# A scan and mixture-of-adapters kernel: the expert weights A move to the load queue, and six warm-up matmuls replace ten

## The chip, the cores and the metric

The kernel runs on one core of a Trainium2 chip. The metric is the device time of one execution in microseconds (us). Five executions of the kernel before took 202.69 to 205.0 us, with a median of 204.11.

## What is computed

The reference runs two steps, one after the other. The first is a linear recurrence along the sequence, for each of 8 batches and 128 channels; the second routes each of the 51,200 resulting rows to the two best of eight small adapters and adds what these return.

```python
# a, b: [8, 6400, 128] float32
for t in range(S):
    h = a[:, t] * h + b[:, t]
    out[:, t] = h
x = out.reshape(51200, 128)
logits = x @ w_gate                    # [N, 8]
topk = indices of the two largest logits of a row
w = softmax over these two
delta = sum over the two of  w * ((x @ A[e]) @ B[e])    # A: [8,128,16], B: [8,16,128]
return x + delta
```

The inputs a and b are 26 MB each, the output is 26 MB; the weights are small (A and B have 64 KB each).

## The kernel before, in words

**Tiling.** The 51,200 rows are cut into 100 blocks of 512 rows, called by their number. For block w, the loads `lda` and `ldb` bring rows of a and b into two rings in SBUF with eight places each (`RING`, L302 and L303). Most loads bring two blocks at once (512 KB); a0, b0, b1 and the last a are alone (256 KB). So a1 means the load of blocks 1 and 2 of a, b2 that of blocks 2 and 3 of b, and so on. One load is one DMA, issued by SyncE (SP), in `load` (L454 to L472).

**One block's way.** TensorE (PE) transposes a and b into PSUM (`A0`, `A1` and `AB<w>`, L492). ScalarE (ACT) copies the transposed a to SBUF (`aev<w>`, L526). VectorE (DVE) runs the recurrence over the 512 columns (`scan<w>`, L550) and leaves x, transposed, as 16-bit numbers in `xT`. PE multiplies x by the joined gate and A weights, `cst_h[:, 0:E_A]` (`ZL<k>`, L589), and ACT copies that to SBUF (`zl<k>`, L607). The gating of a group of blocks (L621 and on) finds the two largest logits and makes the weights. GpSimd (POOL) multiplies the products by these weights (`mul<v>`, L766; DVE for some at the end), PE transposes the result (`T<v>`, L774), ACT or DVE copies it (`tev<v>`, L782), PE adds x and the product with B (`D<v>`, L802), ACT or DVE copies this out of PSUM (`oev<v>`, L817), and SP stores two blocks at a time (`st<j>`, L834 and on). A store also waits until the scan of the block 20 further on is done (`HOLD`). The last two blocks have a store each.

**The order.** No engine's order is written by hand. Each operation is given to a planner (`_Plan`, L64) with an engine, an estimated duration, the operations that it waits for and a key. `schedule` (L89) then walks through an estimated time: at each step it takes, of all operations that could start, the one that can start first, and of equals the one with the lowest key. The result is a fixed list for each engine; `run` (L183) issues it, in order, with semaphore waits. An engine whose next operation waits holds up all that stands behind it in its list. The estimates decide nothing but the order.

DMAs share one estimated link in the planner. A DMA (`add_dma`, L336) has an issue time on its engine, a time `ns` on the link and a time `after` until it counts as landed:

```python
if op.dma:
    link = max(link, free[e] + 550.0) + op.dma[2]      # L154, dma[2] is ns
    end[op.name] = link + op.dma[3]                    # L155, dma[3] is after
```

The planner's clock starts at 700 ns for all engines. A load of 512 KB has 1290 ns on the link, one of 256 KB has 690, the gate weights 80, B 220; a load counts as landed 2000 after its time on the link.

**The head.** ACT issues three small loads before its first other work: the gate weights (`wg_in`), B (`B_in`, 128 rows of 512 bytes) and A (`A_in`, L383 to L394). A is stored as expert, channel, rank and is wanted as channel, expert, rank, so its DMA moves 1,024 pieces of 64 bytes. POOL casts each to 16 bits when it has landed (`cstg`, `cstB`, `cstA`, L419 to L432). All `ZL` wait for `cstg` and `cstA`, besides their scans. After its three DMAs, ACT loads its function table (`table`, L396). Meanwhile PE runs ten matmuls of 512 columns on a zeroed tile whose result nobody reads (`heat`, L399 to L404), and after each of the first five `AB<w>` two more of the same (`fill<w>`, L406). SP issues the loads in the order a0, b0, a1, b1, b2, a3, b4, a5, and so on; their key is `w - 2*RING`, less 200 for w up to 3 (L467).

In the profiled execution, PE runs in the head: `heat`, A0, AB0, fill 0, A1, AB1, fill 1, AB2, fill 2, AB3, ZL0, fill 3, ZL1, AB4.

Of the kernel before, what the change touches and what calls it, by code (L numbers as in the profile page):

```python
# [63 lines left out]
class _Plan:  # L64
# [15 lines left out]
    def add(self, name, eng, kind, unit, busy, emit, deps=(), dma=None, mode=None, takes=(), gives=None):  # L80
        self.ops[name] = _Op(name, eng, kind, unit, busy, self.latency, emit, list(deps), dma, mode, takes, gives)
# [118 lines left out]
def bass_associative_scan_2x2__then__mixture_of_adapters_kernel(  # L200
# [19 lines left out]
    RING = CFG["ring"]  # L220
# [68 lines left out]
    with ExitStack() as stack:  # L289
# [36 lines left out]
        def bank(role):  # L326
            return psum[plan.bank_of[role]]
# [6 lines left out]
        add = plan.add  # L334

        def add_dma(name, eng, unit, starts, slot, ns, deps=(), kind="dma", issue=450.0, after=2000.0):  # L336
# [45 lines left out]
        )  # L382
        add_dma(  # L383
            "A_in",
            "act",
            -108,
            [(cst_f[:, E : E + 128].rearrange("d (e r) -> d e r", e=E), moe_A.rearrange("e d r -> d e r"))],
            ("A",),
            700.0,
            (),  # L390
            "fix",
            450.0,
            5500.0,
        )  # L394
        add("w0", "dve", "fix", -109, 60.0, lambda h: h.memset(warm[:, :], 0.0))
        add("table", "act", "fix", -107, 1500.0, lambda h: h.activation(warm[:, :], warm[:, :], ACTF.Sigmoid), ["w0"])  # L396
        add("wt", "dve", "fix", -109, 60.0, lambda h: h.memset(warm_t[:, :], 0.0))

        def heat(h):  # L399
            for _ in range(10):  # L400
                last = h.matmul(bank(("w", -1))[:, :], warm_t[:, 0:128], warm_t[:, :])
            return last

        add("heat", "pe", "fix", -109, 4000.0, heat, ["wt"], mode="half", takes=[("w", -1)], gives=("w", -1))  # L404

        def fill(w):  # L406

# [521 lines left out]
```

## Time and profile before

| | us |
|---|---|
| median of five executions | 204.11 (202.69 to 205.0) |
| the profiled execution's own time | 204.05 |
| its span, from the first instruction to the last | 202.3 |
| PE, ACT, DVE, POOL busy in it | 182.4, 179.2, 171.8, 157.3 |
| A: issued by ACT, landed | 1.66, 12.11 |
| cast of A on POOL | 12.16 to 12.45 |
| first `ZL` on PE | 12.52 |
| first warm-up matmul, first transpose | 1.22, 4.94 |
| last store issued | 198.15 |

All points in time count from the start of the span. The profile has one row for each group of instructions: line, engine, operation, tiles written and read, how often, and the idle time of the engine just before, with the one that ended it. That one is inferred: where an instruction waits for several, the profile names the one that it holds to be the last. Rows of engines marked with a q, as SPq, are issues of DMAs by the engine's sequencer. The row of a DMA's issue ends long before its data lands; the landing is found from the latency that the profile gives for it.

### The profile page before, as it was taken

To read this page: it belongs to the slowest core of one execution; us is meant where nothing else is said; L and a number is where in the kernel's file an instruction comes from. 1 tells how busy PE (TensorE), PEld (TensorE's weight loads), DVE (VectorE), ACT (ScalarE), POOL (GpSimd) and SP (SyncE) were. 2 spreads that over 40 slices of the span, in tenths; PEclk is the share of its full clock that TensorE was granted. 3 is DMA by queue.
4 is the path that set the end of the run, shared out by engine and by line. 5 is a ranking of instruction groups with operands and counts; after the bars stand their busy time and mean duration, and the time that the engine had idled before them with its cause. 6 is when DMAs were issued, how large, how long until landed. Compare 5 with 4: busy or idle time off the path is not lost.

```text
span 202.3 us, 8187 instructions
## 1 busy us (share of the span) xinstructions
PE 182.4 (90%) x3204; PEld 160.7 (79%) x3204; DVE 171.8 (85%) x296; ACT 179.2 (89%) x461; POOL 157.3 (78%) x280
## 2 busy tenths in 40 slices
PE   7779999998998999997999899989999999998770
PEld 3557788887987988896898799879988989897660
DVE  1469999999999899998879888899799699797970
ACT  2259999999998998998999899999999899999761
POOL 2015568889899697888789799999999999769830
PEclk9999999999999999999999999999999999999999
DMA  6999999999999999999999999999999999986985
GB/s 201 366 410 408 409 405 406 405 407 407 406 419 411 413 415 413 412 411 416 411 410 419 405 413 412 417 411 412 416 412 413 412 414 410 395 341 269 403 337 211
DMA packets 23397, 79.30 MB, mean 392 GB/s; under 512 B 3648, under 2 KB 3776, under 8 KB 23360
## 3 DMA queue, kind: packets, MB, share of 16 engines
q1 hardware_dynamic: 22032, 78.65, 97.4%
q8 instruction: 25, 0.41, 0.8%
q10 hardware_dynamic: 1328, 0.14, 0.5%
q14 instruction: 12, 0.10, 0.1%
HBM read 52.56 MB, written 26.21 MB: 390 GB/s over the span
## 4 chain that ended last, share of the span: by engine, by line
PE 46%; ACT 20%; DVE 10%; issue 7%; DMA 6%; POOL 6%; SPq 2%; DVEq 0%; POOLq 0%
PE ps L492 17%; PE ps L802 14%; PE ps L589 7%; PE ps L774 7%; DMA b_in<-in_b_dram 6%; DVE xT L550 6%; ACT zl L607 6%; ACT a_st L526 6%; POOL zw L766 5%; ACT outt L817 5%; SPq L345 2%; ACT pn L656 2%; DVE zw L766 2%; DVE zwT L782 1%; ACT g L745 1%
## 5 line engine op out<-in xcount | busy, mean ns | idle before, releaser
L550 DVE TENSOR_TENSOR_SCAN xT<-a_st,xT,ps 128x512 f16<-128x512 f32 x96 | 120.2, 1252 | 13.1 <-ACT a_st L526 6.5
L766 POOL TENSOR_TENSOR zw<-zl,g 128x512 f16<-128x512 f32 x93 | 98.7, 1068 | 8.3 <-ACT g L745 8.2
L607 ACT COPY zl<-ps 128x408 f32<-128x408 f32 (+1 forms) x139 | 71.2, 538 | 1.6 <-PE ps L589 1.6
L492 PE MATMUL ps<-ident_f,a_in 64*128 64x64 f32 (+1 forms) x792 | 66.9, 228 | 4.0 <-DMA b_in<-in_b_dram 1.0
L526 ACT COPY a_st<-ps 128x512 f32<-128x512 f32 x100 | 61.2, 637 | 10.0 <-PE ps L492 9.3
L492 PE MATMUL ps<-ident_f,b_in 64*128 64x64 f32 (+1 forms) x792 | 67.1, 228 | 1.7 <-issue 1.6
L492 PEld LDWEIGHTS ps<-ident_f,a_in 64*128 64x128 f32 (+1 forms) x792 | 56.0, 138 | 14.0 <-issue 4.4
L817 ACT COPY outt<-ps 128x512 f32<-128x512 f32 x99 | 60.5, 627 | 2.9 <-PE ps L802 2.3
L492 PEld LDWEIGHTS ps<-ident_f,b_in 64*128 64x128 f32 (+1 forms) x792 | 55.8, 139 | 1.2 <-issue 0.9
L589 PE MATMUL ps<-cst_h,xT 128*128 128x136 f16 x400 | 49.0, 233 | 1.6 <-DVE xT L550 1.5
L802 PE MATMUL ps<-ident_h,xT 128*128 128x128 f16 x400 | 42.9, 229 | 2.3 <-issue 1.3
L774 PE MATMUL ps<-ident_h,zw 128*128 128x128 f16 x400 | 38.7, 220 | 4.2 <-DVE zw L766 2.3
L589 PEld LDWEIGHTS ps<-cst_h,xT 128*128 128x128 f16 x400 | 35.4, 148 | 5.6 <-DVE xT L550 2.1
L782 DVE COPY zwT<-ps 128x256 f32<-128x256 f32 x89 | 35.8, 409 | 3.5 <-PE ps L774 3.3
L802 PE MATMUL ps<-cst_h,zwT 128*128 128x128 f16 x400 | 38.7, 219 | 0.0
L802 PEld LDWEIGHTS ps<-ident_h,xT 128*128 128x128 f16 x400 | 33.2, 148 | 4.7 <-DVE zwT L782 1.9
L774 PEld LDWEIGHTS ps<-ident_h,zw 128*128 128x128 f16 x400 | 25.2, 98 | 7.7 <-DVE zw L766 3.2
L802 PEld LDWEIGHTS ps<-cst_h,zwT 128*128 128x128 f16 x400 | 27.2, 99 | 0.0
L656 ACT ACTIVATE pn<-d 128x96 f32<-128x96 f32 (+2 forms) x72 | 22.9, 328 | 0.1
L735 POOL TENSOR_TENSOR um<-d,pn 128x96 f32<-128x96 f32 (+2 forms) x36 | 14.1, 394 | 5.6 <-ACT pn L656 4.8
L706 POOL TENSOR_TENSOR L<-zl,pn 128x96 f32<-128x96 f32 (+2 forms) x34 | 13.3, 394 | 3.6 <-ACT pn L656 3.0
L728 POOL TENSOR_TENSOR d<-d 128x96 f32<-128x96 f32 (+2 forms) x38 | 13.8, 365 | 1.4 <-DVE d L681 0.5
(31 smaller groups left out, 85.7 us busy)
## 6 DMA issues: line engine op xcount, KB each, us to landing
a_in<-in_a_dram SPq DMA_DIRECT2D x49, 512.0 KB, 15.8
b_in<-in_b_dram SPq DMA_DIRECT2D x49, 512.0 KB, 15.6
out_dram<-outt SPq DMA_DIRECT2D x49, 512.0 KB, 15.5
a_in<-in_a_dram SPq DMA_DIRECT2D x2, 256.0 KB, 9.2
b_in<-in_b_dram SPq DMA_DIRECT2D x2, 256.0 KB, 4.4
out_dram<-outt SPq DMA_DIRECT2D x2, 256.0 KB, 3.6
cst_f<-in_moe_B_dram ACTq DMA_DIRECT2D x1, 64.0 KB, 3.5
cst_f<-in_moe_A_dram ACTq DMA_DIRECT2D x1, 64.0 KB, 10.4
```

Source lines behind the costliest of these rows:

```text
L492: last = h.transpose(*args())
L526: lambda h: h.copy(a_st[w % NAS][:, :], bank(("a", w))[:, :]),
L550: last = h.tensor_tensor_scan(out=x_at(lo, hi), data0=a_st[w % NAS][:, lo:hi], data1=bank(("b", w))[:, lo:hi], initial=init, op0=ALU.mult, ...
L589: last = h.matmul(dst, x_block((b0 + j) // Q, (b0 + j) % Q), wA_h)
L607: return h.copy(zl[:, r0 : r0 + n, :], src)
L656: lambda h: h.activation(v(pn[s]), v(src[s]), ACTF.Relu, bias=bias, scale=scale),
L735: lambda h: h.tensor_tensor(out=v(um[s]), in0=v(d1[s]), in1=v(pn[s]), op=ALU.subtract),
L766: lambda h: h.tensor_tensor(out=oview, in0=zview, in1=gview, op=ALU.mult),
L774: last = h.transpose(dst[:, q * 128 : (q + 1) * 128], zw[v % NZW][:, q, :], ident_h[:, :])
L782: return copy(zwT[v % NZT][:, :].bitcast(F32), bank(("O", v))[:, 0 : UT // 2])
L802: last = h.matmul(bank(("O", v))[:, cols], (x_block(v, q), zwT[v % NZT][:, cols])[part], (ident_h[:, :], Bcat_h)[part], start=part == 0 an ...
L817: return copy(outt[:, v % NOUT, :], bank(("O", v))[:, :])
```

## The change

A is no longer issued by ACT but by SP, in its row of loads. The key puts it between b1 and b2, so it is SP's fifth DMA. The planner is told that A takes 1200 ns on the link instead of 700, and that it counts as landed 2000 after that instead of 5500. The warm-up has six matmuls and not ten, with 2600 ns in the plan instead of 4000. ACT keeps the DMAs of the gate weights and of B. The five fills and all else stay as they are in the program, but the planner makes the order of every engine anew from these numbers.

```diff
         add_dma(
             "A_in",
-            "act",
-            -108,
+            "sp",
+            1.5 - 2 * RING - 200,
             [(cst_f[:, E : E + 128].rearrange("d (e r) -> d e r", e=E), moe_A.rearrange("e d r -> d e r"))],
             ("A",),
-            700.0,
+            1200.0,
             (),
             "fix",
             450.0,
-            5500.0,
+            2000.0,
         )
...
         def heat(h):
-            for _ in range(10):
+            for _ in range(6):
                 last = h.matmul(bank(("w", -1))[:, :], warm_t[:, 0:128], warm_t[:, :])
             return last
...
-        add("heat", "pe", "fix", -109, 4000.0, heat, ["wt"], mode="half", takes=[("w", -1)], gives=("w", -1))
+        add("heat", "pe", "fix", -109, 2600.0, heat, ["wt"], mode="half", takes=[("w", -1)], gives=("w", -1))
```

## The prediction

> **What bounds the kernel now.** I read the page first, then the stretches of busy time, the waits and the timeline of the first 20 us, and last the stores at the end.
>
> ```profile
> PE 182.4 (90%) x3204; PEld 160.7 (79%) x3204; DVE 171.8 (85%) x296; ACT 179.2 (89%) x461; POOL 157.3 (78%) x280
> DMA  6999999999999999999999999999999999986985
> q10 hardware_dynamic: 1328, 0.14, 0.5%
> PE 46%; ACT 20%; DVE 10%; issue 7%; DMA 6%; POOL 6%; SPq 2%; DVEq 0%; POOLq 0%
> ```
>
> The engines and the DMA are both nearly full (the 40 slices fall under 9 in the first and the last few alone), and the chain of waits runs mostly through PE. So the stages have to be told apart; the columns are the stretch, its length, PE, PEld, DVE, ACT and POOL busy, the clock, the DMA share and GB/s:
>
> ```profile
> 20.00:172.00 152.00, 144.44 (x2683) 131.05 (x2682) 138.90 (x226) 146.14 (x374) 134.64 (x231) 1.00 1.03 411
> 172.00:186.00 14.00, 13.35 (x223) 11.99 (x222) 12.12 (x22) 13.75 (x39) 11.16 (x22) 1.00 0.83 332
> 186.00:202.30 16.30, 8.66 (x125) 7.13 (x121) 9.58 (x26) 9.27 (x28) 6.95 (x12) 1.00 0.81 320
> ```
>
> From 20 to 172 us the DMA engines work without a hole at 411 GB/s, and at that rate the 79.3 MB of the page take 193 us by themselves. PE and ACT are 95% and 96% busy beside them. After 20 us the waits name no load. Compute and transfers thus run side by side, and the last stores tell which of them sets the end.
>
> ```profile
> 193.74 0.33 SPq L345 DMA_DIRECT2D out_dram<-outt  x1
> 196.28 0.33 SPq L345 DMA_DIRECT2D out_dram<-outt  x1
> 197.46 0.33 SPq L345 DMA_DIRECT2D out_dram<-outt  x1
> 198.15 0.33 SPq L345 DMA_DIRECT2D out_dram<-outt  x1
> ...
> out_dram<-outt SPq DMA_DIRECT2D x2, 256.0 KB, 3.6
> ```
>
> With their single latencies (5.48, 3.56, 3.64 and 3.59 us) they land at 199.22, 199.84, 201.10 and 201.73: steps of 0.62, 1.26 and 0.63 us for 256, 512 and 256 KB, which is 416 to 423 GB/s, the full rate again. The trace's landing marks (one for each of the 16 DMA engines) say that one engine is late: the first mark of the last store is at 200.6, the last at 201.73, and the slowest engine is behind in this way all through the run. So the end belongs to the slowest DMA engine, and compute has about 1.1 us of slack behind it.
>
> **Where A hurts.** Its row, with the neighbours in time:
>
> ```profile
> 11.35 0.58 ACT L526 COPY a_st<-ps 128x512 f32<-128x512 f32 x1 [0.79 <-PE ps L492]
> 12.16 0.29 POOL L430 CAST cst_h<-cst_f 128x128 f16<-128x128 f32 x1 [7.14 <-DMA cst_f<-in_moe_A_dram]
> 12.52 0.21 PEld L589 LDWEIGHTS ps<-cst_h,xT 128*128 128x128 f16 x2 [1.35 <-DVE xT L550]
> 12.90 0.39 ACT L607 COPY zl<-ps 128x272 f32<-128x272 f32 x1 [0.97 <-PE ps L589]
> 13.35 0.13 PEld L492 LDWEIGHTS ps<-ident_f,a_in 64*128 64x128 f32 x1
> ```
>
> A is issued at 1.66 and lands 10.4 us later, at 12.11. The cast follows, and 0.07 us after it the first products (ZL0). The page puts PE's idle 1.35 us down to the scan, but scan 1 ended at 9.69; the cast of A was the last. PE stood still from 11.3 to 12.5, with ZL0 in front and AB4 (at 13.35, its load in since 11.90) behind.
>
> **The change, part by part.** The sum is made against the profiled execution: 204.05 us, its span of 202.3 and 1.75 around it; the median of the runs shown is 204.11.
>
> *A's bytes.* They are neither more nor fewer. Priced by the dip in the transfers where A's pieces ran:
>
> ```profile
> 5.00:6.00 1.00, 1.00 (x10) 0.90 (x9) 0.00 (x0) 0.43 (x1) 0.01 (x1) 1.00 1.19 288
> 6.00:7.00 1.00, 0.50 (x3) 0.10 (x2) 0.73 (x1) 0.16 (x1) 0.00 (x0) 1.00 1.10 310
> 7.00:8.00 1.00, 0.89 (x11) 0.76 (x12) 0.49 (x1) 0.35 (x1) 0.00 (x0) 1.00 1.04 401
> ```
>
> (411-288)+(411-310) = 224 KB not moved, or 0.54 us; from above, the whole queue q10 (gate, B, A) took 0.5% of 202.3 = 1.0 us. Today these lie beside the loads; after, in their row, ahead of b2. Before and after, every engine moves them once: 0. What no row shows is 1,024 pieces of 64 B inside SP's queue; I bound it by 0.5 us either way (the dip avoided, or paid a second time) and take 0.
>
> *When A lands.* Loads a1 and b1 landed at 6.86 and 7.67 with A beside them; without, up to 0.54 earlier. A follows b1 by 0.54 to 1.0: 7.7 to 8.7, I take 8.3, so cast at 8.65. ZL0 then waits for scan 1 alone, which ends at 9.2 to 9.7. The far end is today's latency from the new issue at 2.54: 12.9.
>
> *SP.* One more issue ahead of b2, some 0.45 us (the row of each early issue), so all later loads are issued 0.45 us later. b2 landed 6.6 us after its issue and the queue only deepens (12.8 us for the load issued at 5.79): hidden by the queue; without that cover, 0.45. ACT loses its third issue: the table load starts at 1.7 in place of 2.15; ACT's next work is at 5.57: 0.
>
> *PE's order.* The planner is given A at 6560+2000 = 8560 (its link sum: a0 2390, gate 2470, b0 3160, B 3380, a1 4670, b1 5360) where it had 5370+5500 = 10870. So ZL0 and ZL1, ready with scan 1 at some 9540 of the plan, come before AB2 (b2 at 9850) and no longer behind AB3. These figures give the order, not a time. On the chip: ZL0 at about 9.4, ZL1 to 9.9, AB2 then at 9.9 in place of 9.22 (0.7 later, with aev2 and scan 2 behind it, now 10.65), AB3 0.5 later, and AB4 at 12.1 instead of 13.35. Scan 4 (14.78, after which DVE is full) moves to about 13.9. What is late next is load b8, which lands at 18.54 and holds AB8 at 18.59; there the scans lose part of the lead. Of 1.2 us I leave 0.8 to products, gating and ACT (full from 20 to 50 us); ends 0 and 1.2.
>
> *Six warm-ups.* Ten took from 1.22 to 4.94; six at 0.43 end at 3.8. a0 landed at 3.71 and b0 at 4.49, so A0 and AB0 can run up to 1.1 and 0.8 us sooner, and scan 0 (6.27) with them. A1 waits for a1 at 6.86 (6.3 after): 0. If the clock stays low longer, the row is the warm-up itself: 634 ns median for it, 379 for the same matmul at L411. PE's 3.7 us of work between 4.9 and 9 (0.60+0.60+0.59+0.71+0.66+0.59 in the timeline) could then take up to 634/379 times as long until the clock comes; most of it fills waits for a1 and b1, and AB1 alone (0.66) and A1 (0.71) move what follows, by some 0.7; scan 1 stays under today's 9.69 plus 0.2, and ZL0 still comes ahead of 12.5. Price 0, ends 0 and 0.7.
>
> The Trainium skill, "TensorE: Matmul & The Clock Gate" (Part 1, the HAM clock gate), speaks against this part: the clock is released after about 3.4 us of sustained activity, counted in free-running windows. By it six warm-ups fall short of a window and ten fill one; AB0 and AB1 would run slow and the sum would be 0.2 to 0.7 us longer in the head. The fall from 634 to 379 ns some 3 us after the first warm-up agrees with the rule; no row shows six.
>
> *To the end.* Compute arrives 0.8 us sooner, but the last three landings follow each other at transfer speed: the slowest engine is not sooner. 0 if it binds as here, 0.8 if it does not; I take 0.2. 204.05 - 0.2 = 203.85, against the median: 203.9.
>
> **The rivals.**
> 1. *The lead is carried to the end*: the constant 3.6 us of the last three stores is a latency and no queue. For it: 15 engines were through up to 1.1 us sooner, and the DMA share after 186 us is 0.81. Against it: steps of exactly 0.62, 1.26, 0.63. Time 204.1 - 0.8 to 1.2 = 203.1, and about 201.9 where the slowest engine is 1.0 less behind too.
> 2. *A late in front of AB2* (the other side): PE works in order, and ZL0 now stands before AB2. It begins with A landing after 9.0 and shows in the time from about 10.2 on, when the 1.1 us of slack are gone. At the far end of 12.9, ZL0 starts at 13.3 and AB2 moves from 9.22 to 13.8; scan 2 follows 1.4 later at 15.2, scans 2 and 3 and the maxima take 3.1, so scan 4 moves from 14.78 to 18.3, and DVE is full after that. 3.5 us, less 1.1: 206.5. For it: A's 10.4 us now. Against it: those were spent beside SP's whole row of loads, while b1, issued in that row at 2.10, took 5.6.
> 3. *The new order is worse further on*: the greedy planner takes all later choices anew. A block costs about 1.8 us of PE (182.4/100); one block's work more exposed at the end, less 1.1 of slack, is +0.7: 204.8; two, +2.5: 206.6. The 7% of issue on the chain shows that order has such a price; nothing shows its sign.
> 4. *Nothing happens in the head either*: A as late, AB2 not blocked: 204.1, inside the forecast.
>
> **How the numbers follow.** Forecast with rival 4: 0.46, own range 203.2 to 204.6. Rival 1: 0.24, of which 0.13 under -1%. Rival 3: 0.17, of which 0.08 over +1%. Rival 2: 0.13, of which 0.08 over. About 1% (202.1 and 206.2) is what a measurement here can tell from no change. Faster 0.13 + 0.02 from the forecast's edge = 0.15; slower 0.08 + 0.08 and 0.03 from the forecast's other edge = 0.19; same 0.66. Range: from rival 1's lower end to rival 3's upper, 202.0 to 206.3.
>
> **What would show it.** Right: A lands at 7.7 to 8.7, ZL0 starts at 9.2 to 9.9, AB4 by 12.3, L401's median stays near 634 and L411 near 379, the last three landings stay 0.6, 1.3, 0.6 apart. Wrong: PE idle before ZL0 past 10.2 with AB2 behind it (rival 2); L411 in the first 10 us over 500 ns (clock); last store issued over 1.1 us after 198.15 (rival 3); an end that moves with the last issue (rival 1); holes in the transfers between 3 and 12 us, which would price A in SP's queue over my 0.5.

## The result, and the profile after

The changed kernel took 203.88 us in the median of 43 runs (203.01 to 207.73), the kernel before, beside it, 203.29 us in 80 runs (202.48 to 207.54). The ratio is 1.0021, with a 95% interval of 1.0005 to 1.0038: by the ratio 0.2% or 0.4 us slower. Times here and below are medians of all executions, while a ratio compares only executions in the faster of two states that the chip shows, and so need not be the quotient of two medians. The profiled execution after took 203.69 us with a span of 201.9.

The head did what the change says, and more. From the trace's timeline (start, duration, engine, line):

```profile
2.57 0.43 SPq L345 DMA_DIRECT2D cst_f<-in_moe_A_dram  x1
7.36 0.29 POOL L430 CAST cst_h<-cst_f 128x128 f16<-128x128 f32 x1 [2.33 <-DMA cst_f<-in_moe_A_dram]
9.04 0.35 PE L589 MATMUL ps<-cst_h,xT 128*128 128x136 f16 x2 [1.03 <-DVE xT L550]
13.78 1.26 DVE L550 TENSOR_TENSOR_SCAN xT<-a_st,xT,ps 128x512 f16<-128x512 f32 x1
```

A landed 4.7 us after its issue, at 7.31 instead of 12.11. ZL0 now waits for scan 1 (`xT L550`), no longer for A. Scan 4 (the last line) started 1.0 us sooner than before.

The end did not come sooner. The page:

```profile
PE 183.7 (91%) x3200; PEld 162.4 (80%) x3200; DVE 171.3 (85%) x294; ACT 180.7 (89%) x463; POOL 158.1 (78%) x280
...
PEclk9999999999969999999999999999999999999998
DMA  6999999999999999999999999999999999987977
...
q8 instruction: 25, 0.41, 0.8%
q10 hardware_dynamic: 288, 0.07, 0.2%
...
PE 44%; ACT 17%; DVE 11%; DMA 8%; POOL 7%; issue 7%; SPq 4%; POOLq 1%; ACTq 0%; DVEq 0%
```

Queue q10 has lost A (1328 packets before, 288 now). New is the 6 in the clock's row, at 55 to 60 us. The long stretch is as full as it was (the stretch, its length, PE, PEld, DVE, ACT, POOL, clock, DMA share, GB/s):

```profile
20.00:172.00 152.00, 145.31 (x2666) 131.78 (x2665) 137.94 (x225) 145.65 (x370) 133.88 (x229) 0.99 1.03 412
172.00:186.00 14.00, 12.98 (x216) 11.61 (x213) 13.19 (x22) 13.71 (x37) 11.09 (x20) 1.00 0.82 327
186.00:201.90 15.90, 8.45 (x128) 7.26 (x125) 8.13 (x25) 9.80 (x30) 7.65 (x14) 0.96 0.84 329
```

The last stores show that the bound has changed:

```profile
195.97 0.33 SPq L345 DMA_DIRECT2D out_dram<-outt  x1
197.36 0.33 SPq L345 DMA_DIRECT2D out_dram<-outt  x1
197.85 0.35 SPq L345 DMA_DIRECT2D out_dram<-outt  x1
198.34 0.67 SPq L345 DMA_DIRECT2D out_dram<-outt  x1
```

They landed at 198.63, 200.03, 200.70 and 201.37, after 2.67 to 3.03 us, and all 16 DMA engines were done with the last one within 0.2 us. Before, the last store was issued at 198.15, took 3.59 us, and one engine came 1.1 us after the first. So the slow DMA engine no longer holds the end; compute does, and it issued its last store 0.19 us later than before. The lead of the head (scan 10 started 1.02 us sooner, scan 20 0.70; scans are counted from 0 as DVE runs them, and four blocks have two) is not there at the end. Where it went can't be read scan by scan against before: the two orders place the scans differently, and from scan 30 on the difference swings between 1.60 us sooner and 2.30 late. Comparisons within one order, further down, are steady. In the chain of waits from 50 to 62 us (start, length, what):

```profile
53.53 1.51 PE ps L492 x39
55.04 1.45 issue
56.49 0.52 PE ps L492 x9
```

PE stood for 1.45 us in the middle of one AB, between two transposes of the same block, where the program has no wait.

### The profile page after: what moved, and what is told of

It is laid out like the page before. It is cut to its first block, busy times and chain, and to the rows that moved or that the text cites. A ratio compares the mean times of both kernels' runs of the same rounds, so it can differ in the third digit from the quotient of the medians.

```text
span 201.9 us, 8170 instructions
## 1 busy us (share of the span) xinstructions
PE 183.7 (91%) x3200; PEld 162.4 (80%) x3200; DVE 171.3 (85%) x294; ACT 180.7 (89%) x463; POOL 158.1 (78%) x280
## 4 chain that ended last, share of the span: by engine, by line
PE 44%; ACT 17%; DVE 11%; DMA 8%; POOL 7%; issue 7%; SPq 4%; POOLq 1%; ACTq 0%; DVEq 0%
PE ps L492 16%; PE ps L802 13%; DVE xT L550 8%; PE ps L589 8%; DMA a_in<-in_a_dram 8%; PE ps L774 7%; ACT outt L817 5%; ACT zl L607 5%; POOL zw L766 5%; ACT a_st L526 4%; SPq L345 4%; ACT pn L656 2%; ACT g L745 1%; DVE zwT L782 1%; POOLq L289 1%
## 5 line engine op out<-in xcount | busy, mean ns | idle before, releaser
L550 DVE TENSOR_TENSOR_SCAN xT<-a_st,xT,ps 128x512 f16<-128x512 f32 x96 | 120.2, 1252 | 10.5 <-ACT a_st L526 5.8
L607 ACT COPY zl<-ps 128x408 f32<-128x408 f32 (+1 forms) x139 | 73.1, 536 | 2.8 <-PE ps L589 2.4
L492 PE MATMUL ps<-ident_f,a_in 64*128 64x64 f32 (+1 forms) x792 | 68.0, 230 | 2.5 <-DMA a_in<-in_a_dram 1.1
L492 PE MATMUL ps<-ident_f,b_in 64*128 64x64 f32 (+1 forms) x792 | 68.3, 230 | 1.4 <-issue 1.4
L492 PEld LDWEIGHTS ps<-ident_f,a_in 64*128 64x128 f32 (+1 forms) x792 | 56.6, 140 | 11.6 <-issue 3.3
L817 ACT COPY outt<-ps 128x512 f32<-128x512 f32 x100 | 61.3, 624 | 2.8 <-PE ps L802 1.7
L492 PEld LDWEIGHTS ps<-ident_f,b_in 64*128 64x128 f32 (+1 forms) x792 | 56.7, 140 | 2.2 <-issue 1.9
L589 PE MATMUL ps<-cst_h,xT 128*128 128x136 f16 x400 | 50.7, 235 | 1.9 <-DVE xT L550 1.5
L589 PEld LDWEIGHTS ps<-cst_h,xT 128*128 128x128 f16 x400 | 36.4, 148 | 5.9 <-DVE xT L550 2.6
L698 POOL TENSOR_TENSOR d<-zl,m 128x96 f32<-128x96 f32 (+2 forms) x34 | 11.7, 343 | 4.1 <-DVE m L691 3.8
```

Source lines behind the costliest of these rows:

```text
L492: last = h.transpose(*args())
L550: last = h.tensor_tensor_scan(out=x_at(lo, hi), data0=a_st[w % NAS][:, lo:hi], data1=bank(("b", w))[:, lo:hi], initial=init, op0=ALU.mult, ...
L589: last = h.matmul(dst, x_block((b0 + j) // Q, (b0 + j) % Q), wA_h)
L607: return h.copy(zl[:, r0 : r0 + n, :], src)
L817: return copy(outt[:, v % NOUT, :], bank(("O", v))[:, :])
```

## The experiments

Each ratio is against the kernel before, run beside it on the same chip. "Old order" means that all engines keep the order of the kernel before, "new order" that of the changed kernel.

### The transfers, the warm-ups and the order apart

One line at the end of `schedule` moves A between queues and leaves the order of everything else. In the old order:

```diff
+        self.order["act"].remove(ops["A_in"]); self.order["sp"].insert(4, ops["A_in"]); ops["A_in"].eng = "sp"
...
-            for _ in range(10):
+            for _ in range(6):
```

`oldorder_sp_6` has both edits, `oldorder_sp_10` the first alone, `oldorder_act_6` the second alone.

> The old order of every engine, with A's DMA moved to SP as its fifth and six warm-ups: the change without the planner's new order. Theory O (the new order loses the lead of the head): A lands at about 7.3 as in the changed kernel, PE does not stop before the first products, and the lead of up to 1 us stays: 0.2 to 0.6% faster than before (ratio 0.994 to 0.998). Rival Q (A in SP's row of loads costs): as slow as the changed kernel or slower, ratio 1.002 or more. Rival W (six warm-ups cost): the same 1.002, with slow matmuls in the first 10 us. If the end belongs to the slowest DMA engine alone: 1.000.

> The old order with A's DMA on SP and the ten warm-ups kept. Theory O: as the run with six warm-ups, ratio 0.994 to 0.998, since the first transposes wait for load a1 anyway. Rival W: faster than the one with six by 0.2% or more. Rival Q: 1.002 or more.

> The old order with A on ACT as before, and six warm-ups. Theory O: 1.000 (0.999 to 1.001), the first transposes start 1 us sooner and wait for load a1 again. Rival W: 1.002 or more, with the clock low in parts of the first 10 us.

Measured: 203.12 us (ratio 0.9972, 0.9934 to 1.001), 202.98 (0.9977, 0.9939 to 1.0015) and 203.02 (0.9974, 0.9931 to 1.0017). Neither A's 1,024 pieces in SP's row nor the six warm-ups cost anything that can be measured, and both at once bring no gain that can be either: all three intervals hold 1. `oldorder_sp_10` shows why: it issued its last store at 197.03, 1.1 us sooner than before, but that store took 4.5 us and landed at 201.53, 0.2 us sooner. (`oldorder_act_6` differs here: issued 1.32 us sooner than before, its last store landed 1.29 us sooner, with one engine 1.15 us behind the first.) The page of `oldorder_sp_10`, KB and us from issue to landing:

```profile
out_dram<-outt SPq DMA_DIRECT2D x2, 256.0 KB, 4.5
```

The new order with the old transfers, A third on ACT and ten warm-ups:

```diff
+        self.order["sp"].remove(ops["A_in"]); self.order["act"].insert(2, ops["A_in"]); ops["A_in"].eng = "act"
...
-            for _ in range(6):
+            for _ in range(10):
```

> The changed kernel's order of every engine, but A issued by ACT as its third DMA and ten warm-ups: the new order without the change. A lands at about 12 and the first products, now ahead of block 2's transposes on PE, start at about 12.5; block 2's transposes start at 13 instead of 9.2. Theory O: slower than before by the order's cost (0.2%) and by the stop of PE, less what the slack takes: ratio 1.005 to 1.015. Rival Q or W: no worse than 1.000 to 1.005, since neither A in SP's row nor six warm-ups are in it.

Measured: 210.88 us, but with runs from 203.29 to 212.08, so that no interval is given. A took 11.0 us on ACT's queue and landed at 12.71:

```profile
12.76 0.29 POOL L430 CAST cst_h<-cst_f 128x128 f16<-128x128 f32 x1 [7.51 <-DMA cst_f<-in_moe_A_dram]
13.20 0.42 PE L589 MATMUL ps<-cst_h,xT 128*128 128x136 f16 x2 [4.04 <-POOL cst_h L430]
```

PE stood for 4.04 us with ZL0 in front and AB2 behind it, and then ran at half its clock (same columns as above; the clock is third from the end):

```profile
13.20:19.00 5.80, 5.80 (x56) 3.83 (x58) 2.65 (x6) 2.65 (x7) 0.70 (x3) 0.50 1.02 409
```

This is rival 2, and PE's stop in the head is real. What it costs is not measured: the profiled execution (212.08 us) is the longest of the six, another took 203.29, and the same order with ten warm-ups and A early (`neworder_sp_10`, below) took 206.7 by itself.

### What the planner is told

The same program, where A's `after` is 2000 (the changed kernel once more), 3000, 3900 or 4600. Only the order differs; 4600 gives the old order, and so the same program as `oldorder_sp_6`.

```diff
-            2000.0,
+            3000.0,
```

> The changed kernel unaltered, beside three that differ from it in one number of the planner alone. Theory O (the new order loses the head's lead): 1.002 against before, and 0.3 to 0.6% slower than told_4600, whose DMAs and matmuls are the same. Rival Q (A in SP's row of loads costs): all four of this call at 1.002 or more. Rival N (nothing but the run's scatter): all four alike within 0.2%.

> The changed kernel with the planner told that A lands 3000 after its time on the link and not 2000: same DMAs, same instructions; the order of PE has block 2's transposes ahead of the first products, and everything later is planned anew. Theory O in its narrow form (what costs is the head, the first products ahead of block 2): as told_4600, 0.997. Theory O in its wide form (each order has its own pauses far behind the head): a value of its own between 0.995 and 1.005, that need not lie between its neighbours'.

> As before with 3900: block 2's transposes and its two fills ahead of the first products, block 3's behind. Narrow form: as told_4600, 0.997. Wide form: a value of its own between 0.995 and 1.005.

> As before with 4600: the planner then gives every engine the very order of the kernel before, so that this is the change without a new order (the program of oldorder_sp_6, measured once more beside the changed kernel). Theory O: 0.995 to 0.999, faster than after_again by 0.3 to 0.6%, the lead of about 1 us kept to the last store's issue wherever the clock stays full. Rival Q or N: as after_again, 1.002.

Measured: 203.70 (1.0032, 1.0 to 1.0064), 203.81 (1.0011, 0.9987 to 1.0035), 206.41 (1.0134, 1.0088 to 1.018) and 203.32 (1.0004, 0.998 to 1.0028). With equal work and equal transfers, an order alone came to ratios of 1.0004 to 1.0134; only `told_3900`, outside both its expectations, is clear of the others, and between the changed kernel's repetition and `told_4600` the intervals overlap. In the profiled execution of `told_3900` (209.42 us, the longest of its six), PE paused for 1.59 us at 17.3 (for a load of b), and for 1.54 and 1.51 us at 79.2 and 95.6, and stretches at half clock followed the first two.

### Does the slowest DMA engine hold the end?

Stores 12, 20, 28 and 36 are cut to 64 columns (the rest of their rows is not written); this takes 1.97 MB, or 4.8 us at 411 GB/s, off the DMA engines and nothing off compute. The edit, in the kernel before, in `told_4600` and in the changed kernel:

```diff
+            if j in (12, 20, 28, 36):
+                rows, tile = rows[:, 0:64], tile[:, 0:64]
```

> The kernel before, with four of its 51 stores (j = 12, 20, 28, 36) cut from 1024 to 64 columns; the rest of those rows is not written. Orders of all engines are before's. It spares the DMA engines 1.97 MB, 4.8 us at 411 GB/s, and no engine of compute anything. If the slowest DMA engine sets the end of before and compute has 1.1 us of slack behind it, the time falls by 0.5 to 1.1 us and not by 4.8, and the last store then lands under 3.1 us after its issue. If compute sets the end already, it stays within 0.3 us.

> Before's order with A in SP's row and six warm-ups, and the same four stores cut to 64 columns. Its profile without the cut had the last store issued 3.0 us sooner than before and landed 1.1 us sooner. If the slowest DMA engine holds the end there, the time falls by 1 to 2.5 us against its own 203.1 to 203.3 and comes out at 200.5 to 202.3, ratio 0.985 to 0.994. If the end is set by compute and the late engine only goes with it, it stays at 203.

> The changed kernel (new order) with the same four stores cut to 64 columns. If its end is set by compute, as the late issues and the latencies of 2.7 to 3.0 us in its two profiles say, it stays at 203.4 to 203.9, ratio 1.001 to 1.003, and the gap to before's order with the same cut opens from 0.4 to 1 us or more. If the DMA engines set its end, it falls by 1 to 2 us too.

Measured: 202.83 us (0.9937, 0.9897 to 0.9976), 200.64 (0.9867, 0.9821 to 0.9913) and 203.73 (0.9981, 0.9942 to 1.0019). `told_4600` is the clear case; its last store without and with the cut:

```profile
195.18 1.24 SPq L345 DMA_DIRECT2D out_dram<-outt  x1
...
195.12 0.33 SPq L345 DMA_DIRECT2D out_dram<-outt  x1
```

The first landed at 200.59, the second at 197.73. First the page without the cut:

```profile
out_dram<-outt SPq DMA_DIRECT2D x2, 256.0 KB, 5.4
```

and with it:

```profile
out_dram<-outt SPq DMA_DIRECT2D x2, 256.0 KB, 2.3
```

Its scans start within 0.1 us of each other in the two, from scan 38 to the last. So compute had 3 us of lead at its end, and the slowest DMA engine (2.7 us behind the first without the cut) kept 2.9 of them. `before_light` landed 1.37 us sooner than before, 0.97 of it from a latency of 2.62 for 3.59: the slack of about 1.1 us that I had read from before was there.

`after_light` was to stay at the time of the changed kernel. The gap to the old order of `told_4600` did open, from 0.2 or 0.3% to 1.1% (0.4% to `before_light`): with the load taken off the DMA engines, the new order's compute is the later one. But it fell a little too, and its trace shows one reason: its last store was issued at 195.92, 2.4 us sooner than in the changed kernel. (This profiled execution, 201.42 us, is the fastest of twelve, which go up to 204.86.) From 50 to 75 us, the first of PE's waits in the changed kernel (us in all, times, longest):

```profile
PE ps L492 <- issue: 1.4, 1, 1.4
PE ps L774 <- issue: 0.7, 1, 0.7
PE ps L492 <- ACT zl L607: 0.3, 1, 0.3
```

and in `after_light`:

```profile
PE ps L589 <- ACT outt L817: 0.9, 1, 0.9
PE ps L774 <- issue: 0.6, 1, 0.6
PE ps L492 <- ACT zl L607: 0.3, 1, 0.3
```

The pause of 1.45 us is missing, and it had come before any cut store (the first was issued at 87.7 us). Of five profiles of this program's order with six warm-ups and whole fills, four have the pause at 55 us, of 1.43 to 1.45 us; `after_light` alone does not. These five have one order, so their scans can be compared one by one. Against `after_light`, the changed kernel is 0.06 us late at scan 29 (50.4 us), 2.32 at scan 39 (68.1 us) and 2.43 at the last; its repetition is 0.13, 2.11 and 2.17 late. Nearly the whole loss falls at the pause and in the 12 us behind it.

### What the pauses are

From 45 us on and up to the last stretch, PE's pauses of over 0.6 us lie at fixed places in its list. Counted in recorded matmuls, the changed kernel has them at 838 and 1087, its repetition at 838 and 962; before at 715, 963, 1460, 1833; `told_3900` at 964, 1088, 1212, 1460 (put down to a scan), 1584, 2330. That is every 123 to 125 matmuls, or a multiple. Old and new orders share these places, and four warm-ups more do not move them: before, with ten, has its pause at 715 inside the 457th matmul of L492, `oldorder_act_6`, with six, at 715 inside the 461st. The page shows 25 packets of kind "instruction" with 0.41 MB, 16 KB each, over 3,200 recorded matmuls with a weight load each: 128 to a packet. In the changed kernel one packet's transfer ends at 55.14, and the pause runs from 55.04 to 56.49; in `told_3900` packets end at 79.41 and 95.78, and the pauses run from 79.21 to 80.75 and from 95.64 to 97.15. The same holds throughout: over all twenty profiles, 47 pauses of more than 0.6 us between 45 and 186 us have no releaser named, and every one ends 1.20 to 1.62 us after the end of such a packet's transfer. So I took the pauses for PE waiting for its next 16 KB of instructions. If that is so, more matmuls in the head move the places in the work. First, the changed kernel with ten warm-ups and the plan of six:

```diff
-            for _ in range(6):
+            for _ in range(10):
```

> The changed kernel with ten warm-ups in the program, while the planner keeps the 2600 ns of six: the orders of all engines stay the changed kernel's. If the order is what costs, it stays at 203.6 to 204.0, ratio 1.001 to 1.004. If the six warm-ups cost, it falls to before's 203.3 or under. PE has four instructions more ahead of everything; if PE's pause of 1.4 us at 55 us, seen in both profiles of the changed order, belongs to the place in PE's list of instructions, it moves by some matmuls or stays within 1 us of 55; if it is chance, it is gone.

Measured: 206.7 us (1.0165, 1.0116 to 1.0215), a miss: the order is the changed kernel's, and A is early. PE's pauses in its timeline:

```profile
56.55 0.27 PE L492 MATMUL ps<-ident_f,b_in 64*128 64x64 f32 x1 [0.95 <-issue]
...
64.52 0.38 PE L802 MATMUL ps<-cst_h,zwT 128*128 128x128 f16 x4 [1.05 <-issue]
...
72.60 0.27 PE L802 MATMUL ps<-cst_h,zwT 128*128 128x128 f16 x2 [1.11 <-issue]
80.41 0.21 PE L492 MATMUL ps<-ident_f,a_in 64*128 64x64 f32 x1 [1.62 <-issue]
```

They come after matmuls 838, 962, 1087 and 1211 of PE's list. The first is at the 520th matmul of L492 and no longer at the 524th: four more warm-ups, four matmuls earlier in the work, and the same place in the list. After the fourth pause, the clock was at half from 81.7 to 85.1. By scan 50 (88.9 us) this run was 3.35 us behind before and 2.40 behind the changed kernel, which has its order.

Two kernels tried to take load off the DMA engines altogether, with stores 0 to 43 cut (`if j < 44`; the rest of those rows is not written):

> The changed kernel with stores 0 to 43 cut from 1024 to 64 columns; the rest of those rows is not written, the last seven stores are whole. Orders of all engines are the changed kernel's. It takes about 21 MB of 79 off the DMA engines and nothing off compute. Theory: PE's pauses are late fetches of its instructions, which wait behind data in the DMA engines; with a quarter of the data gone, the pauses at the fetches (55.0, 63.6, 71.6 us) shrink under 0.4 us, no stretch at half clock follows, and the last store is issued at 193 to 196 in place of 198.3. Rival: the planner's order is worse by what waits for what; then the last store stays over 1 us later than in before's order with the same cut.

> Before's order with A in SP's row and six warm-ups, and the same stores 0 to 43 cut to 64 columns (the rest of those rows is not written). If fetches and the clock make the difference between the two orders, its last store is issued within 0.7 us of that of the changed kernel with the same cut; if the order itself does, it is issued 1 to 2.5 us sooner than there.

Measured: 205.86 us (1.0138, 1.0087 to 1.0189) and 201.33 (0.9866, 0.9811 to 0.9921), four runs each. The first expectation fell: with a quarter of the bytes gone, the pause at 838 is still 1.45 us, and the last store was issued at 198.14, against 198.34 whole. So compute, and not the amount of data, sets that order's last issue; that the packets wait behind the stores' data is not borne out. Its last three stores then took 4.4 to 4.7 us to land, which I can't explain. The profile of `old_fewstores` has 6.83 us at half clock from 7.9 us on and is not compared; the times of the two, 4.5 us apart, say again that without the stores' load the new order is the slower one.

Next, 64 empty instructions ahead of PE's list, in the changed kernel and in `told_4600`:

```diff
+        for _ in range(64 if eng == "pe" else 0):
+            handle.nop()
```

> The changed kernel with 64 empty instructions ahead of PE's list; orders and work are the same, but every later place in PE's instruction memory moves by 64 instructions. If PE's pauses are fetches of 16 KB, they stay at fixed distances in the list and so come some 24 to 32 matmuls (1 to 2 us of work) earlier in the work: the pause after PE's matmul 838 goes, and there is one at about 806 to 814. The time changes with it, by up to 3 us either way. If the pauses belong to the work (a wait in the order that the profile does not show), they stay at 838 and 962 and the time at 203.7 to 203.9.

> Before's order with A in SP's row and six warm-ups, and the same 64 empty instructions ahead of PE's list. If the place of the fetches in the work decides what an order costs, this one's time of 203.1 to 203.3 may rise too, to as much as 206; if before's order bears any place of them because compute leads the DMA engines by 1 to 3 us, it stays at 202.9 to 203.5.

Measured: 204.24 us (1.0031, 0.9995 to 1.0068) and 203.29 (1.0016, 0.9985 to 1.0048). The pause of 1.45 us stayed at matmul 838 and at the same transpose. By the expectation that speaks for a wait that belongs to the work; but the packets also end at the same matmuls as before (838, 957, 1079 beside 838, 959, 1079 in the repetition), so nothing was moved, and whether the empty instructions reached PE's memory no row shows. The two tell nothing about the pauses. So the last pair moves real matmuls: in the five fills, eight of 128 columns replace two of 512.

```diff
-                for _ in range(2):
-                    last = h.matmul(bank(("w", w))[:, :], warm_t[:, 0:128], warm_t[:, :])
+                for i in range(8):
+                    last = h.matmul(bank(("w", w))[:, 0:128], warm_t[:, 0:128], warm_t[:, 0:128])
```

> The changed kernel; each of the five fills has eight matmuls of 128 columns in place of two of 512, so 30 matmuls more on PE in the head for the same columns; orders as in the changed kernel. If PE's pauses are its 16 KB instruction packets, they stay at PE's matmuls 838, 962, 1087 of the list, which are then 30 matmuls earlier in the work (the pause now inside the 524th matmul of L492 comes at its 496th to 508th), and with another place the time may leave 203.9: 202.9 to 206.7. If they belong to the work, they stay at the 524th matmul of L492, and the time at 203.7 to 203.9.

> Before's order with A in SP's row and six warm-ups, and the same five fills of eight matmuls of 128 columns. Its compute is 3 us ahead of before at the last store and the DMA engines end it, so pauses that move should not show: 202.9 to 203.5. If the place of the packets decides for this order too, it goes to 204 or more.

Measured: 203.82 us (1.0027, 0.9993 to 1.006) and 204.47 (1.0051, 1.0018 to 1.0085). In the profiles the roles are exchanged; in the times, the old order lost (1.0051, where it stood at 1.0004 and 0.9972 with whole fills), but the new one did not gain. In the new order the pause at 55 us is gone. PE's waits of that kernel from 50 to 86 us begin with:

```profile
PE ps L492 <- issue: 0.5, 1, 0.5
```

It issued its last store at 196.05, and the DMA engines ended it (4.63 us to land, the slowest engine 1.8 behind). The old order got the pauses, after matmuls 840, 1088 and 1336; they stand in its chain of waits:

```profile
54.04 1.42 issue
...
69.27 1.37 issue
...
83.34 1.74 issue
```

`told_4600` had one pause of 0.69 us in that stretch, and was 2.04 us ahead of before at scan 50; this one was 2.75 us behind, and issued its last store at 198.34 in place of 195.18. Against `told_4600`, which has the same order, its scans are 0.76 us late ahead of the first of these pauses, 2.0 behind it, 3.0 behind the second and 4.8 behind the third. The places in PE's list are those of all other kernels (840 is within the few records that a trace lacks), and the work at them is other work. This shows that the pauses go with PE's list of instructions and not with the order's waits. That they are the packets' landing rests on the spacing and the times given above. From the start of a packet's transfer to the end of the pause, the 47 took 2.27 to 2.65 us, so a packet comes late when its transfer starts with less work than that left in front of its place: at matmul 815 to 819 for place 838 in the four profiles with the pause, at 788 in `after_light`. What sets the start is open.

Ten of the profiles together, with the start of a scan less that of before, and the last store (for the kernels with the new order, the scans 40, 50 and last compare only with each other):

| kernel | scan 10 | scan 20 | scan 40 | scan 50 | last scan | last store issued | landed |
|---|---|---|---|---|---|---|---|
| before | 0 | 0 | 0 | 0 | 0 | 198.15 | 201.73 |
| changed | -1.02 | -0.70 | -0.03 | +0.94 | +0.08 | 198.34 | 201.37 |
| changed, again | -0.68 | -0.35 | -0.24 | +0.67 | -0.19 | 198.09 | 201.12 |
| `after_light` | -0.73 | -0.43 | -2.35 | -1.43 | -2.35 | 195.92 | 198.95 |
| `after_fill8` | -0.27 | -0.12 | -2.27 | -2.60 | -2.23 | 196.05 | 200.68 |
| `neworder_sp_10` | -0.02 | -0.02 | +0.04 | +3.35 | +2.71 | 200.98 | 204.01 |
| `told_4600` | -1.53 | -1.28 | -1.92 | -2.04 | -2.95 | 195.18 | 200.59 |
| `oldorder_sp_6` | -1.38 | +0.30 | +0.74 | +0.62 | -0.15 | 197.99 | 201.17 |
| `oldorder_act_6` | -0.75 | -0.74 | -0.46 | -0.58 | -1.32 | 196.83 | 200.44 |
| `old_fill8` | -1.22 | -0.40 | +0.07 | +2.75 | +0.24 | 198.34 | 201.57 |

`oldorder_sp_6` and `told_4600` are one and the same program. The first paused for 1.12 us at 18.05 (for a load of a), ran at half clock from 20.9 to 24.3 and paused for 1.13 us at matmul 715, where the second did not; its last store was issued 2.8 us later and landed 0.6 us later. So one profile is not its kernel: a single execution of the same program moves by nearly as much as the orders differ, and in the old order most of that is hidden at the end.

## Why the prediction was right and where it was wrong

**Right: the head.** A was to land at 7.7 to 8.7 and landed at 7.31, just ahead of the range. ZL0 was to start at 9.4 (9.2 to 9.9) and started at 9.04, AB4 at 12.1 and started at 12.14, scan 4 at 13.9 and started at 13.78. AB2 was to be held until 9.9 and came at 9.32. Where these differ, the chip was sooner: a1 landed 1.0 us and b1 0.8 us earlier than before. That this is due to A, which no longer ran beside them, is not shown: over all profiles a1 landed at 5.7 to 7.9 us with A in SP's row and at 6.1 to 7.2 with A on ACT.

**Right: A's bytes, SP and the warm-ups at 0.** Three kernels in the old order stand at 0.997 with these edits, and a repetition of the one with both at 1.0004. The Trainium skill's "TensorE: Matmul & The Clock Gate" (Part 1, the HAM clock gate) spoke against six warm-ups. The clock did come later, at 5.9 us instead of 4.4 in the two profiles, and the first fill matmul took 558 ns, over the 500 that I had set as a sign; the other nine took 379 to 390. Over all profiles the full clock came at 4.2 to 7.2 us with six warm-ups and at 4.4 to 6.6 with ten. `oldorder_act_6` has the six alone, with its first two fill matmuls at 634 ns, and shows no cost.

**Right for the old order: the slowest DMA engine.** A lead of 1.1 us at the last issue gave 0.2 us at the end (`oldorder_sp_10`), one of 3.0 gave 1.1 (`told_4600`), and without the four stores 2.62 us of lead over `before_light` gave 2.63. `oldorder_act_6` kept its 1.32 all the same: in the old order the slowest engine is 0.6 to 2.7 us behind, from one profile to the next, so rival 1, the lead carried to the end, is weakened and not out. In the changed kernel the sign failed: the last landings are 1.40, 0.67 and 0.67 apart, and not 0.6, 1.3 and 0.6, as they follow issues 1.39, 0.49 and 0.49 apart.

**Wrong: the lead of 0.8 us after load b8, and with it "to the end I take 0.2".** I let compute keep 0.8 us and asked only whether the DMA engines would take it. In the profile, compute kept nothing. It lost 2.4 us at and after the pause at matmul 838 (last issue 198.34 against 195.92 without it). The DMA engines by themselves end at 200.6 (`told_4600`, `after_fill8`; 200.4 to 201.7 in others that they end), and a last store in this order takes 3.0 us to land, so compute binds from an issue at 197.6 on: 1.7 us of slack without the pause, 0.7 too late with it. The old order of `told_4600` needs 2.6 us for its last store and so binds from 198.0 on; issued at 195.18, it has 2.8 us and can bear one such pause, as `oldorder_sp_6` did. So the sign was missed: rival 3, the new order worse further on, is what happened, at +0.4 us where I had priced it at +0.7. Its cause was not the one that I named. I spoke of a block's work more exposed by the planner's later choices, about 1.8 us; what the profiles show is PE's list with other work at the places where PE stops. My sign for rival 3, a last issue over 1.1 us after 198.15, was set for an end that the DMA engines hold, and missed it: the issue moved by 0.19. That the time itself, 203.9, came out at 203.88 is luck: I had summed from 204.05 and the median of five executions, 204.11, where before's median over 80 is 203.29. The 7% of "issue" in the chain was the row that had it, and I took it for a price of order in general without looking at where its pieces lie.

**What stays open.** The changed kernel, its repetition and `after_shift` stand at 1.0021 to 1.0032, the five in the old order with whole fills at 0.9972 to 1.0016, with intervals that overlap. That the pauses make the whole difference is not shown: `after_fill8` had no pause like it at 55 us in its profile and yet a ratio of 1.0027 over its runs, and without the pause the new order's last issue is still 0.7 and 0.9 us behind that of `told_4600`, so that a part may be the order itself, as rival 3 has it. A profile is one execution, and the pauses and the clock change from one to the next.

## What to carry to other kernels

When two bounds lie within 1 us of each other, ask not only what a change gives to one, but how much of its slack the other order has left: a lead that is not seen at the end still pays for the next stall. An edit that makes a planner choose anew, or adds four matmuls in the head, changes what PE is doing where its instruction list stalls, and that can be worth more (here up to 1.6%) than the edit; so try the edit with the old order kept, and try several orders. PE's "issue" pieces in the chain are worth counting by their place in PE's list before a change is priced.

## What the hardware showed beside that

The same A took 4.6 to 6.6 us in SP's row in all kernels that had it there, and 9.7 to 11.0 us on ACT's queue beside the loads. PE's clock went to half for 3.41 us, or twice that, after some pauses of 0.9 to 4.0 us and not after others, one of 1.74 us (`old_fill8`) among them. In the changed kernel, by stretches with the clock third from the end:

```profile
55.00:56.50 1.50, 0.05 (x4) 0.01 (x2) 1.37 (x2) 0.78 (x3) 1.50 (x3) 1.00 1.02 404
...
57.00:58.00 1.00, 1.00 (x13) 1.00 (x13) 0.54 (x2) 0.59 (x1) 0.78 (x2) 0.56 1.04 422
58.00:59.00 1.00, 1.00 (x12) 1.00 (x11) 1.00 (x1) 0.69 (x2) 0.91 (x2) 0.50 1.02 418
59.00:60.00 1.00, 1.00 (x16) 0.81 (x16) 0.99 (x3) 0.80 (x2) 0.88 (x1) 0.50 1.02 414
```

Its repetition had the same pause (1.43 us) and no such stretch, and lost nearly as much, 2.1 us against 2.3 at scan 39: most of it is not the clock's.
